# The opening schedule of a recurrent-attention and feed-forward kernel: first chunk in another order

## The chip, the cores and the metric

The kernel runs on one core of one Trainium2 chip. The metric is device time in microseconds (us) of one execution; lower is better. The kernel before takes 201.43 us, the median of three runs (201.3 to 201.53). The profiled execution has a span of 199.0 us, and all times of the trace count from its start.

## What is computed

For each of 4 batches and 8 heads the reference keeps a 48x48 state and walks through 768 steps:

```python
for t in range(S):                         # r, k, v: [4, 8, 768, 48]
    cur   = einsum('bhd,bhe->bhde', u * k_t, v_t)
    y[t]  = einsum('bhd,bhde->bhe', r_t, state + cur)
    state = w * state + einsum('bhd,bhe->bhde', k_t, v_t)
x   = y as [3072, 384]
h   = x @ w_in                             # [384, 2048]
out = (h * sigmoid(h)) @ w_out             # [2048, 384]
```

The kernel cuts the 768 steps into 6 chunks of 128. One chunk of one batch is a **unit**: unit i is chunk i // 4 of batch i % 4, so there are 24, and units 0 to 3 are the first chunk, which has no state to start from.

## The kernel before

Work on one unit goes through all engines. In program names, with the short words that the schedule uses (i is the unit):

- loads `rin`, `kin`, `vin` (`lr`, `lk`, `lv`): 192 KB each, four buffers of each kind;
- `TR`, `TK`: TensorE transposes r and k into the accumulator `att`; `rT`, `kT`: VectorE multiplies them by powers of w; `A`: TensorE forms the 128x128 products of each head; `am`: VectorE masks them;
- `ku`, `ru`: GpSimd forms k*u and r*k*u; `rd`: VectorE sums that over each head; `vu`: v times the sum, on VectorE for units 0 to 3 and on GpSimd from unit 4 on; `kc`: GpSimd's decayed k; `sd`: GpSimd's decayed state;
- `Y`: TensorE's output into `yp`; `y16`: VectorE adds `vu` and frees `yp`; `S`: TensorE's new state into `sp`; `st`: the state is put away (ScalarE for units 0 to 3, VectorE later); `stb`: GpSimd's 16-bit copy;
- `yT`, `xT`: y transposed, and copied for the feed-forward part; `L`: six TensorE matmuls with `win` into `hps`; `G`: ScalarE's silu; `i_q`, `i_o`: GpSimd asks for quarters of `win` and `wout`.

`wb`, `ub` spread the rows w and u over 128 partitions with a matmul; `ubc` copies the second into `u_bc`.

```python
att = [ps.tile([128, 2, 512], FP, name=f"att{i}") for i in range(2)]
def next_att():                            # the two accumulators take turns
    turns.append(0)
    return att[len(turns) % 2]
...
nc.scalar.dma_start(out=u_row, in_=...u as one row...)
nc.scalar.dma_start(out=w_row, in_=...w as one row...)
for i in range(B):
    for dst, src in ((rin, r), (kin, k), (vin, v)):
        ld(i, dst, src, nc.scalar if i < 2 and dst is kin else nc.sync)
...
spins = [0]
def spin(ps_tile):                         # matmuls of zeros, for nothing but to keep TensorE at work
    for _ in range(spins[0]):
        nc.tensor.matmul(ps_tile, idle[:, 0:128], idle[:, 0:ps_tile.shape[-1]], start=True, stop=True)
    spins[0] = 0
...
yp, sp, hps, ops, yT, bc:  ps.tile(..., tag="moe", bufs=4)    # four PSUM banks for all of them
```

The opening is a written list; each word is one step, and a number with a star gives the zero matmuls ahead of it. Each engine runs its own share of the list in this order:

```python
order = """
    lnw 5*TR0 eK lamK rT0 8*TK0 v160 ub kT0 A0 ubc i_q0 v161 wb am0 ku0 TR1 lnwb TK1 lamC
    rT1 Y0 i_q1 kT1 ru0 lr4 4*A1 v162 i_q2 rd0 TR2 vu0 TK2 kc0 lk4 lv4 y160 am1 ku1 yT0 S0
    ... (cut: units 1 to 5) ...
    yT4 yT5 G2.14 ru6 xT4 xT5 kc7 rd6 vu6 ku7 ru7 stb4 rd7 stb5 vu7 v167
"""
```

After it a loop takes two units at a time; `fill(n)` sets n pieces of feed-forward work between the steps:

```python
for i in range(6, 24, 2):
    product_pair(i)                        # A of units i and i+1
    for n in (i + 2, i + 3):
        bonus_products(n)                  # ku, ru on GpSimd
        decayed_k(n)                       # kc on GpSimd
    masked(i); masked(i + 1)               # am on VectorE
    fill(4)
    outputs(i); evict_y(i); turn_y_dma(i); state(i); state16(i)      # Y S, y16, xT, st, stb
    fill(2)
    outputs(i + 1); evict_y(i + 1); turn_y_dma(i + 1); state(i + 1); state16(i + 1)
    ...
    fill(2)
    for n in (i + 2, i + 3): turn(n); decay(n)
    for n in (i + 2, i + 3): bonus_sum(n); cast_v(n); bonus_v(n); decayed_state(n)   # rd, v16, vu, sd
    ...
```

Of the kernel before, what the change touches and what calls it, by code (L numbers as in the profile page):

```python
# [8 lines left out]
FP = mybir.dt.float32  # L9
# [6 lines left out]
def kernel(  # L16
# [11 lines left out]
    nc = tc.nc  # L28

    B, H, S, D = r.shape  # L30
    C = 128
    NCH = S // C
    HD = H * D
    NP = H // 2
# [9 lines left out]
    cst = ctx.enter_context(tc.tile_pool(name="cst", bufs=1))  # L44
# [9 lines left out]
    turns = []  # L54

    def next_att():
        turns.append(0)
        return att[len(turns) % 2]
# [12 lines left out]
    def ld(i, dst, src, eng=nc.sync):  # L71
        sc, b = unit(i)
        eng.dma_start(
            out=dst[i % NIN][:, :, 0:D],
            in_=src[b, :, sc * C:sc * C + C, :].rearrange("h t d -> t h d"))
# [19 lines left out]
                      in_=bass.AP(tensor=src.tensor, offset=D * j, ap=[[1, D], [PW, NP]]))  # L95

    w_row = cst.tile([1, HD], FP)
    u_row = cst.tile([1, HD], FP)
    ones = cst.tile([1, 128], FP)
    idle = cst.tile([128, 512], F16)  # L100
    nc.scalar.preload_act_table_set("natural_log_exp_and_others")
# [1 line left out]
    nc.vector.memset(idle, 0.0)  # L103
    columns(nc.sync, wpT, w, 1)
    columns(nc.scalar, wpT, w, 0)
    nc.scalar.dma_start(out=u_row, in_=bass.AP(tensor=u.tensor, offset=0, ap=[[0, 1], [1, HD]]))
    nc.scalar.dma_start(out=w_row, in_=bass.AP(tensor=w.tensor, offset=0, ap=[[0, 1], [1, HD]]))
    for i in range(B):
        for dst, src in ((rin, r), (kin, k), (vin, v)):
            ld(i, dst, src, nc.scalar if i < 2 and dst is kin else nc.sync)  # L110
    nc.vector.memset(ones, 1.0)
    for i in range(NIN):
        nc.vector.memset(rin[i][:, :, D:64], 0.0)
# [32 lines left out]

    spins = [0]

    def spin(ps_tile):
        for _ in range(spins[0]):  # L150
            nc.tensor.matmul(ps_tile, idle[:, 0:128], idle[:, 0:ps_tile.shape[-1]],  # L151
                             start=True, stop=True)
        spins[0] = 0

# [12 lines left out]

    spread = {}

    def spread_row(key, row):  # L170
        spread[key] = ps.tile([128, HD], FP, name="bc", tag="moe", bufs=4)
        nc.tensor.matmul(spread[key], ones, row, start=True, stop=True)  # L172

    def ln_w():
        nc.scalar.activation(out=lnw_bc, in_=spread["w"], func=AF.Ln)
# [4 lines left out]
        nc.scalar.activation(out=wCT, in_=lnwT, func=AF.Exp, scale=float(C))  # L180
        nc.scalar.preload_act_table_set("silu_and_others")

    def copy_u():
        nc.scalar.copy(out=u_bc.rearrange("p h d -> p (h d)"), in_=spread["u"])  # L184
        nc.scalar.copy(out=maskX[0:HC, :], in_=maskM[HC:C, :])
        nc.scalar.copy(out=maskX[HC:C, :], in_=maskM[0:HC, :])

# [2 lines left out]
    def L(i):  # L190
        return live.setdefault(i, {})
# [45 lines left out]

    def turn_one(i, x):
        if x == 0:
            t = next_att()  # L240
            spin(t[:, 0, :])
            L(i)["t"] = t.rearrange("p y (x g t) -> p y x g t", x=2, g=NP)
        else:
            spin(L(i)["t"][:, 0, 1].rearrange("p g t -> p (g t)"))
        flat = (rin, kin)[x][i % NIN].rearrange("p h d -> p (h d)")
        for p in range(NP):
            for y in range(2):
                rows = slice(HC * y, HC * y + HC)
                nc.tensor.transpose(L(i)["t"][0:PR, y, x, p, :], flat[rows, 128 * p:128 * p + PR],  # L249
                                    ident[rows, rows])  # L250
# [19 lines left out]
        nc.scalar.copy(out=L(i)["rT16"], in_=L(i)["rT"])  # L270

    def product(i):
        at = next_att()
        spin(at[:, 0, :])
        a = L(i)["a"] = at.rearrange("p j (g c) -> p j g c", g=NP)
        rT, kT = L(i)["rT"], L(i)["kT"]
        for p in range(NP):
            for j, r0 in ((0, 0), (1, 64)):
                nc.tensor.matmul(a[:, j, p, :], kT[r0:r0 + D, p, :], rT[r0:r0 + D, p, :],  # L279
                                 start=True, stop=True)  # L280
# [16 lines left out]
    def masked(i):  # L297
        am = L(i)["am"] = wrk.tile([128, 2, NP, C], F16, name="am")
        nc.vector.tensor_tensor(  # L299
            out=am.rearrange("p h g c -> p (h g) c"), in0=L(i)["a"].rearrange("p h g c -> p (h g) c"),  # L300
            in1=(maskX if crossed(i) else maskM).unsqueeze(1).broadcast_to([128, H, C]), op=ALU.mult)

    def outputs_y(i):
        sc, b = unit(i)
        yp = ps.tile([128, 512], FP, name="yp", tag="moe", bufs=4)
        spin(yp)
        L(i)["y"] = yp[:, 0:HD].rearrange("p (h d) -> p h d", h=H)
        for p in range(NP):
            if sc:
                nc.tensor.matmul(L(i)["y"][:, 2 * p:2 * p + 2, :],  # L310
                                 L(i)["rT16"][0:PR, p, :],
                                 st16[b][:, p, :], start=True, stop=False)
            for j in range(2):
                h = 2 * p + j
                nc.tensor.matmul(L(i)["y"][:, h, :], L(i)["am"][:, j, p, :], L(i)["vy"][:, h, :],  # L315
                                 start=not sc, stop=(not sc or j == 1))
# [74 lines left out]
    def l1_mm(sc, b0, nb, ft):  # L391
        m = B // nb
        hps = hpss[b0, ft] = ps.tile([128, m, nb * C], FP, name="hps", tag="moe", bufs=4)
        spin(hps.rearrange("p m c -> p (m c)"))
        for f in range(m):
            for q in range(NQ):
                nc.tensor.matmul(hps[:, f, :], win[:, q, (ft + f) * 128:(ft + f + 1) * 128],  # L397
                                 xts[sc][:, q, b0:b0 + nb, :].rearrange("p b t -> p (b t)"),
                                 start=(q == 0), stop=(q == NQ - 1))
# [37 lines left out]
    def fill(n):  # L437
        for _ in range(n):
            if fillers:
                fillers.pop(0)()  # L440
# [14 lines left out]
    def piece(word, f):  # L455
# [2 lines left out]

    steps = {
        "lnw": powers_r, "eK": exponents_k, "lamK": powers_k,  # L460
        "wb": lambda: spread_row("w", w_row), "ub": lambda: spread_row("u", u_row),
        "lnwb": ln_w, "lamC": powers_c, "ubc": copy_u,
    }
    unit_steps = {
        "TR": lambda i: turn_one(i, 0), "TK": lambda i: turn_one(i, 1),
        "rT": lambda i: decay_one(i, 0), "kT": lambda i: decay_one(i, 1),
        "A": product, "am": masked, "v16": cast_v, "kc": decayed_k,
        "vu": lambda i: bonus_v_rows(i) if i < B else bonus_v(i),
# [4 lines left out]
        "osb": lambda b: store(0, b),  # L473
    }
    order = """
        lnw 5*TR0 eK lamK rT0 8*TK0 v160 ub kT0 A0 ubc i_q0 v161 wb am0 ku0 TR1 lnwb TK1 lamC
        rT1 Y0 i_q1 kT1 ru0 lr4 4*A1 v162 i_q2 rd0 TR2 vu0 TK2 kc0 lk4 lv4 y160 am1 ku1 yT0 S0
        xT0 st0 ru1 lr5 kT2 2*Y1 rT2 1*TR3 kc1 lk5 rd1 1*A2 vu1 lv5 ku2 S1 y161 st1 ru2 lr6 am2
        yT1 xT1 kc2 lk6 rd2 3*Y2 L0.0 vu2 lv6 sd4 S2 G0.0 y162 L0.2 sd5 st2 rT3 yT2 L0.4 ku3 TK3
        G0.2 L0.6 kT3 G0.4 ru3 lr7 L0.8 G0.6 A3 i_q3 rd3 G0.8 vu3 xT2 i_o0 TR4 v163 am3 TK4 kc3  # L480
        lk7 lv7 L0.10 v164 kT4 G0.10 Y3 kc4 S3 y163 st3 TR5 rT4 ku4 yT3 TK5 rT5 xT3 ru4 r164
        L2.0 kT5 r165 L2.2 kc5 rd4 G2.0 A45 G2.2 vu4 ku5 L2.4 am4 L2.6 G2.4 ru5 am5 Y4 G2.6 S4
        sd6 L0.12 v165 y164 L2.8 sd7 st4 TR6 i_o1 G0.12 rd5 Y5 S5 G2.8 rT6 TK6 vu5 L0.14 st5
        r166 i_o2 L2.10 G0.14 y165 i_o3 kT6 G2.10 L2.12 v166 kc6 TR7 TK7 G2.12 rT7 L2.14 ku6 kT7
        r167 yT4 yT5 G2.14 ru6 xT4 xT5 kc7 rd6 vu6 ku7 ru7 stb4 rd7 stb5 vu7 v167
    """
    for word in order.split():
        if "*" in word:
            n, word = word.split("*")
            spins[0] = int(n)  # L490
        if word == "A45":
            product_pair(4)
        elif word in steps:
            steps[word]()
        elif word[0] == "L":
            piece(word[1:], l1_mm)
        elif word[0] == "G":
            piece(word[1:], l1_silu)
        elif word[0] == "M":
            l2_mm(0, int(word[1]), int(word[3]))  # L500
        else:
            unit_steps[word[:-1]](int(word[-1]))
# [5 lines left out]
    for i in range(B + 2, NU, 2):  # L508
        sc, b = unit(i)
        nxt = range(i + 2, min(i + 4, NU))  # L510
        product_pair(i)
        for n in nxt:
            bonus_products(n)
            decayed_k(n)
        masked(i)
        masked(i + 1)
        fill(4)
        outputs(i)
        evict_y(i)
        turn_y_dma(i)  # L520
        state(i)
        state16(i)
        fill(2)
        outputs(i + 1)
        evict_y(i + 1)
        turn_y_dma(i + 1)
        state(i + 1)
        state16(i + 1)
        if b:
            fillers.extend((first(sc) if sc > 1 else rest_first(sc)) + second(sc))  # L530
        fill(2)
        for n in nxt:
            turn(n)
            decay(n)
        load(i + NIN)
        load(i + 1 + NIN)
        for n in nxt:
            bonus_sum(n)
            cast_v(n)
            bonus_v(n)  # L540
            decayed_state(n)
        for n in nxt:
            fill(2)
            cast_r(n)
        fill(4)
# [31 lines left out]
```

## Time and profile before

| what | value |
|---|---|
| time, median of 3 | 201.43 us |
| span of the profiled execution | 199.0 us |
| TensorE (PE) busy | 188.1 us, 95% |
| GpSimd (POOL) busy | 117.7 us, 59% |
| ScalarE (ACT) busy | 107.9 us, 54% |
| VectorE (DVE) busy | 102.6 us, 52% |
| zero matmuls before 52.5 us | 24, 8.2 us busy |
| from 52.5 to 195.6 us (143.1 us): PE busy | 143.0 us |
| last matmul ends, last copy ends | 195.5 us, 196.1 us |

How to read it: a matmul's record overlaps that of its neighbour, so 95% does not mean that no time can be gained, and the zero matmuls count as busy. The line to keep in mind is the one from 52.5 us on: there one TensorE instruction follows the other until the end. What can be won or lost lies ahead of that point, or in new holes after it.

### The profile page before, as it was taken

What the parts mean: (1) busy time and instruction counts of PE and PEld (TensorE: products, weight loads), DVE (VectorE), ACT (ScalarE), POOL (GpSimd) and SP (SyncE); (2) the same over time, 40 slices, a digit from 0 to 9 for tenths busy, and PEclk for the clock granted to TensorE, in tenths of its full rate; (3) what the DMA queues carried; (4) which work ended last, traced back from release to release, by engine and by line L of the source; (5) the groups of instructions that cost most, each with busy time, mean ns of one, the idle gap of its engine ahead of it and who ended that gap; (6) DMA issues with size and microseconds to landing.
All of it is one profiled execution on the core that took longest, in us unless ns stands there. A gap on an engine that the chain in (4) does not pass through costs nothing.

```text
span 199.0 us, 5520 instructions
## 1 busy us (share of the span) xinstructions
PE 188.1 (95%) x2254; PEld 122.4 (61%) x2254; DVE 102.6 (52%) x176; ACT 107.9 (54%) x216; POOL 117.7 (59%) x151
## 2 busy tenths in 40 slices
PE   5899798989799999999999999999999999999992
PEld 2466476878676688666646756547665566644551
DVE  6229979673772782763564554646635625000121
ACT  5255478678572076073794355792436880179300
POOL 8079897889989919839839649569468030000000
PEclk9999999999999999999999999999999999999999
DMA  5999999899149258279175386291395102310022
GB/s 97 238 186 199 198 198 185 173 165 180 16 94 245 83 127 172 65 156 219 26 145 113 82 187 174 46 199 38 85 216 141 40 3 59 104 40 0 0 79 79
DMA packets 89981, 24.15 MB, mean 121 GB/s; under 512 B 83298, under 2 KB 89956, under 8 KB 89956
## 3 DMA queue, kind: packets, MB, share of 16 engines
q1 hardware_dynamic: 83952, 20.26, 46.7%
q0 software_dynamic: 3712, 3.15, 10.5%
q10 hardware_dynamic: 2292, 0.40, 1.0%
q8 instruction: 17, 0.28, 0.6%
q14 instruction: 8, 0.07, 0.1%
HBM read 20.45 MB, written 4.72 MB: 126 GB/s over the span
## 4 chain that ended last, share of the span: by engine, by line
PE 76%; POOL 16%; issue 4%; DVE 1%; ACT 1%; POOLq 0%; DVEq 0%
PE ops L418 32%; PE hps L397 25%; PE att L292 6%; PE att L249 5%; POOL kc L207 4%; POOL ku L199 4%; POOL rku_f L203 2%; PE yp L315 2%; POOL sdec L338 2%; PE yp L310 2%; PE bc L172 2%; POOL wout L89 2%; PE sp L327 1%; PE att L279 1%; PE att L151 1%
## 5 line engine op out<-in xcount | busy, mean ns | idle before, releaser
L397 PE MATMUL hps<-xT,win 128*128 128x256 f16 (+1 forms) x384 | 66.9, 326 | 0.4 <-ACT xT L385 0.4
L418 PE MATMUL ops<-wout,gT 128*128 128x384 f16 x384 | 65.8, 326 | 0.0
L405 ACT ACTIVATE gT<-hps 128x512 f16<-128x512 f32 x96 | 55.0, 604 | 18.3 <-PE hps L397 16.2
L418 PEld LDWEIGHTS <-gT 128*128 128x128 f16 x384 | 36.2, 98 | 23.1
L397 PEld LDWEIGHTS <-win 128*128 128x128 f16 x384 | 35.8, 98 | 23.0 <-issue 0.4
L299 DVE TENSOR_TENSOR am<-att,maskM 128x1024 f16<-128x1024 f32 x14 | 17.1, 1222 | 35.1 <-PE att L292 31.9
L424 ACT COPY osb<-ops 128x384 f32<-128x384 f32 x20 | 9.6, 480 | 45.2 <-PE ops L418 45.2
L223 POOL TENSOR_TENSOR vu<-vin,rku 128x384 f32<-128x384 f32 x20 | 16.5, 830 | 28.8 <-DVE rku L218 22.2
L199 POOL TENSOR_TENSOR ku<-kin,u_bc 128x384 f32<-128x384 f32 x24 | 24.4, 1018 | 5.8 <-ACT u_bc L184 5.4
L203 POOL TENSOR_TENSOR rku_f<-rin,ku 128x384 f32<-128x384 f32 x24 | 24.5, 1019 | 1.8
L207 POOL TENSOR_TENSOR kc<-kin,lamC 128x384 f16<-128x384 f32 x24 | 24.0, 1003 | 0.7 <-ACT wCT L180 0.7
L255 DVE TENSOR_TENSOR rT<-att,lamR 112x512 f32<-112x512 f32 x24 | 16.5, 686 | 11.6 <-PE att L249 7.4
L343 DVE TENSOR_TENSOR y<-yp,vu 128x384 f16<-128x384 f32 x24 | 13.3, 556 | 13.1 <-POOL ku L199 4.7
L255 DVE TENSOR_TENSOR kT<-att,lamK 112x512 f32<-112x512 f32 x24 | 16.3, 680 | 3.5 <-PE att L249 3.5
L292 PEld LDWEIGHTS att<-rT,kT 48*64 48x64 f32 x640 | 14.5, 133 | 3.3 <-issue 2.8
L292 PE MATMUL att<-rT,kT 48*64 48x64 f32 (+1 forms) x640 | 16.1, 247 | 0.0
L426 DVE COPY osb<-ops 128x384 f32<-128x384 f32 x4 | 2.2, 558 | 25.0 <-PE ops L418 25.0
L218 DVE TENSOR_REDUCE rku<-rku_f 128x8 f32<-128x384 f32 x24 | 12.4, 543 | 3.5 <-POOL rku_f L203 3.5
L338 POOL TENSOR_TENSOR sdec<-st,wCT 112x384 f32<-112x384 f32 x16 | 13.5, 846 | 0.4 <-ACT st L358 0.4
L270 ACT CAST rT<-rT 112x512 f16<-112x512 f32 x20 | 12.4, 623 | 0.9 <-DVE rT L255 0.8
L315 PEld LDWEIGHTS <-am 128*128 128x128 f16 x192 | 9.7, 98 | 4.8 <-DVE am L299 3.2
L299 DVE TENSOR_TENSOR am<-att,maskX 128x1024 f16<-128x1024 f32 x10 | 12.1, 1214 | 0.0
(63 smaller groups left out, 179.3 us busy)
## 6 DMA issues: line engine op xcount, KB each, us to landing
rin<-in_r_dram SPq DMA_DIRECT2D x24, 192.0 KB, 3.6
vin<-in_v_dram SPq DMA_DIRECT2D x24, 192.0 KB, 3.8
out_dram<-osb SPq DMA_DIRECT2D x24, 192.0 KB, 2.7
kin<-in_k_dram SPq DMA_DIRECT2D x22, 192.0 KB, 3.6
win<-in_moe_w_in_dram POOLq DMA_DIRECT2D x4, 384.0 KB, 6.5
wout<-in_moe_w_out_dram POOLq DMA_DIRECT2D x4, 384.0 KB, 8.2
kin<-in_k_dram ACTq DMA_DIRECT2D x2, 192.0 KB, 4.8
xT<-y SPq DMA_TRANSPOSE x18, 2.3
```

Source lines behind the costliest of these rows:

```text
L199: nc.gpsimd.tensor_tensor(out=L(i)["ku"], in0=kin[i % NIN][:, :, 0:D], in1=u_bc, op=ALU.mult)
L203: nc.gpsimd.tensor_tensor(out=L(i)["rku_f"], in0=rin[i % NIN][:, :, 0:D], in1=L(i)["ku"], op=ALU.mult)
L207: nc.gpsimd.tensor_tensor(out=kc[i % NIN][:, :, 0:D], in0=kin[i % NIN][:, :, 0:D], in1=lamC, op=ALU.mult)
L223: nc.gpsimd.tensor_tensor(out=L(i)["vu"], in0=vin[i % NIN], in1=L(i)["rku"].unsqueeze(2).broadcast_to([128, H, D]), op=ALU.mult)
L255: nc.vector.tensor_tensor(out=L(i)[key].rearrange("p g (y t) -> p y g t", y=2), in0=L(i)["t"][0:PR, :, x], in1=lam.rearrange("p g (y t) -> ...
L292: nc.tensor.matmul(a[e][o0:o0 + HC, j, p, c0:C], kT[r0:r0 + D, p, s0:s0 + HC], rT[r0:r0 + D, p, c0:C], start=True, stop=True)
L299: nc.vector.tensor_tensor(out=am.rearrange("p h g c -> p (h g) c"), in0=L(i)["a"].rearrange("p h g c -> p (h g) c"), in1=(maskX if crossed ...
L315: nc.tensor.matmul(L(i)["y"][:, h, :], L(i)["am"][:, j, p, :], L(i)["vy"][:, h, :], start=not sc, stop=(not sc or j == 1))
L338: nc.gpsimd.tensor_tensor(out=L(i)["sdec"], in0=st[b], in1=wCT.unsqueeze(2).broadcast_to([PR, NP, PW]), op=ALU.mult)
L397: nc.tensor.matmul(hps[:, f, :], win[:, q, (ft + f) * 128:(ft + f + 1) * 128], xts[sc][:, q, b0:b0 + nb, :].rearrange("p b t -> p (b t)"), ...
L405: nc.scalar.activation(out=gts[sc][:, ft:ft + m, b0 * C:(b0 + nb) * C], in_=hpss[b0, ft], func=AF.Silu)
L418: nc.tensor.matmul(opss[b], gts[sc][:, ft, b * C:(b + 1) * C], wout[:, ft, :], start=(ft == 0), stop=(ft == NFT - 1))
```

## The change

It rearranges the opening. r and k of a unit are transposed by one step, `T`. The table of u is loaded with 128 copies by a DMA straight into `u_bc` (192 KB on the queue of ScalarE) instead of one row, a matmul and a copy; so GpSimd's `ku` can begin without TensorE. On that queue v of unit 0 takes the place of k of unit 0. The zero matmuls go into the accumulator that `next_att` will hand out next, ahead of the step, and 21 of them stand in the list instead of 24 (9 ahead of `T0`, 6 ahead of `A0`). The first three quarters of `win` are asked for after `ku` and `ru` of units 0 and 1. Almost every step changes its place. And `rd` and `vu` of units 6 and 7 leave the list: they come in the loop's first round, after the masks.

```diff
-    u_row = cst.tile([1, HD], FP)
-    nc.scalar.dma_start(out=u_row, in_=bass.AP(tensor=u.tensor, offset=0, ap=[[0, 1], [1, HD]]))
+    nc.scalar.dma_start(out=u_bc, in_=bass.AP(tensor=u.tensor, offset=0,
+                                              ap=[[0, 128], [D, H], [1, D]]))
...
-            ld(i, dst, src, nc.scalar if i < 2 and dst is kin else nc.sync)
+            by_act = (i == 0 and dst is vin) or (i == 1 and dst is kin)
+            ld(i, dst, src, nc.scalar if by_act else nc.sync)
...
-    def spin(ps_tile):
+    def spin():
         for _ in range(spins[0]):
-            nc.tensor.matmul(ps_tile, idle[:, 0:128], idle[:, 0:ps_tile.shape[-1]],
+            nc.tensor.matmul(att[(len(turns) + 1) % 2][:, 0, :], idle[:, 0:128], idle,
                              start=True, stop=True)
...
     order = """
-        lnw 5*TR0 eK lamK rT0 8*TK0 v160 ub kT0 A0 ubc i_q0 v161 wb am0 ku0 TR1 lnwb TK1 lamC
-        rT1 Y0 i_q1 kT1 ru0 lr4 4*A1 v162 i_q2 rd0 TR2 vu0 TK2 kc0 lk4 lv4 y160 am1 ku1 yT0 S0
-        ... (cut)
+        lnw eK lamK 9*T0 ku0 v160 kT0 ru0 lr4 rT0 6*A0 ku1 rd0 vu0 v161 ru1 wb am0 T1 lr5 lnwb
+        i_q0 lamC kT1 2*Y0 i_q1 y160 1*T2 kc0 lk4 lv4 rT1 yT0 xT0 rd1 1*A1 i_q2 v162 vu1 kc1 lk5
+        lv5 S0 st0 am1 ku2 S1 kT2 st1 Y1 ru2 lr6 y161 rT2 1*T3 yT1 kc2 lk6 xT1 rd2 1*A2 vu2
+        lv6 ku3 S2 L0.0 am2 st2 ru3 lr7 L0.2 kc3 lk7 kT3 Y2 G0.0 L0.4 y162 G0.2 sd4 L0.6 rT3
+        G0.4 yT2 rd3 sd5 G0.6 A3 xT2 sd6 L0.8 am3 v163 mx L0.10 G0.8 vu3 lv7 i_q3 Y3 G0.10 S3
+        i_o0 y163 T4 st3 yT3 kT4 kc4 xT3 rT4 ku4 v164 L2.0 r164 L2.2 ru4 G2.0 T5 G2.2 kc5 L2.4
+        rd4 kT5 L2.6 G2.4 vu4 rT5 A45 G2.6 ku5 r165 ru5 L0.12 am4 L2.8 G0.12 sd7 am5 Y4 G2.8 S4
+        L0.14 v165 y164 L2.10 st4 L2.12 i_o1 rd5 G0.14 Y5 vu5 T6 G2.10 S5 G2.12 i_o2 y165 L2.14
+        v166 st5 yT4 i_o3 G2.14 yT5 kT6 xT4 kc6 rT6 xT5 r166 T7 ku6 kT7 ru6 rT7 r167 kc7 ku7 ru7
+        stb4 stb5 v167
     """
...
         masked(i)
         masked(i + 1)
+        if i == B + 2:
+            bonus_sum(i)
+            bonus_v(i)
+            bonus_sum(i + 1)
+            bonus_v(i + 1)
         fill(4)
```

More of the change, by code (lines that the diff above doesn't have):

```diff
@@ L168, with spread_w @@
     spread = {}
-    def spread_row(key, row):
-        spread[key] = ps.tile([128, HD], FP, name="bc", tag="moe", bufs=4)
-        nc.tensor.matmul(spread[key], ones, row, start=True, stop=True)
+    def spread_w():
+        spread["w"] = ps.tile([128, HD], FP, name="bc", tag="moe", bufs=4)
+        nc.tensor.matmul(spread["w"], ones, w_row, start=True, stop=True)
     def ln_w():
@@ L181, in powers_c, with cross_mask @@
         nc.scalar.preload_act_table_set("silu_and_others")
-    def copy_u():
-        nc.scalar.copy(out=u_bc.rearrange("p h d -> p (h d)"), in_=spread["u"])
+    def cross_mask():
         nc.scalar.copy(out=maskX[0:HC, :], in_=maskM[HC:C, :])
@@ L239, in turn_one @@
         if x == 0:
[L240 to L244, printed above, removed]
+            L(i)["t"] = next_att().rearrange("p y (x g t) -> p y x g t", x=2, g=NP)
         flat = (rin, kin)[x][i % NIN].rearrange("p h d -> p (h d)")
@@ L272, in product @@
     def product(i):
-        at = next_att()
-        spin(at[:, 0, :])
-        a = L(i)["a"] = at.rearrange("p j (g c) -> p j g c", g=NP)
+        a = L(i)["a"] = next_att().rearrange("p j (g c) -> p j g c", g=NP)
         rT, kT = L(i)["rT"], L(i)["kT"]
@@ L305, in outputs_y @@
         yp = ps.tile([128, 512], FP, name="yp", tag="moe", bufs=4)
-        spin(yp)
         L(i)["y"] = yp[:, 0:HD].rearrange("p (h d) -> p h d", h=H)
@@ L393, in l1_mm @@
         hps = hpss[b0, ft] = ps.tile([128, m, nb * C], FP, name="hps", tag="moe", bufs=4)
-        spin(hps.rearrange("p m c -> p (m c)"))
         for f in range(m):
@@ L460 @@
         "lnw": powers_r, "eK": exponents_k, "lamK": powers_k,
-        "wb": lambda: spread_row("w", w_row), "ub": lambda: spread_row("u", u_row),
-        "lnwb": ln_w, "lamC": powers_c, "ubc": copy_u,
+        "wb": spread_w,
+        "lnwb": ln_w, "lamC": powers_c, "mx": cross_mask,
     }
     unit_steps = {
-        "TR": lambda i: turn_one(i, 0), "TK": lambda i: turn_one(i, 1),
+        "T": turn,
         "rT": lambda i: decay_one(i, 0), "kT": lambda i: decay_one(i, 1),
@@ L475 @@
     order = """
-        lnw 5*TR0 eK lamK rT0 8*TK0 v160 ub kT0 A0 ubc i_q0 v161 wb am0 ku0 TR1 lnwb TK1 lamC
-        rT1 Y0 i_q1 kT1 ru0 lr4 4*A1 v162 i_q2 rd0 TR2 vu0 TK2 kc0 lk4 lv4 y160 am1 ku1 yT0 S0
[L478 to L485, printed above, removed]
+        lnw eK lamK 9*T0 ku0 v160 kT0 ru0 lr4 rT0 6*A0 ku1 rd0 vu0 v161 ru1 wb am0 T1 lr5 lnwb
[8 more added lines that the diff above has]
+        stb4 stb5 v167
     """
@@ L490 @@
             spins[0] = int(n)
+            spin()
         if word == "A45":
```

## The prediction

> **What bounds the kernel now.** I read the page's slices first: PE shows nines almost everywhere, so I asked where TensorE truly waits. The list of waits, restricted to PE after 52.5 us, is empty; so nothing after that point can be gained, and the question is when that gapless stretch begins.
>
> ```profile
> PE   5899798989799999999999999999999999999992
> POOL 8079897889989919839839649569468030000000
> DMA  5999999899149258279175386291395102310022
> ```
>
> A slice is 5 us. In the first ten POOL is at 7 to 9 and the DMA engines at 8 or 9. The chain that ended last, in order of time, says who ruled: GpSimd from 15 us to 50 us, and then this:
>
> ```profile
> 48.49 0.96 POOL ku L199
> ...
> 49.53 1.01 POOL rku_f L203
> 50.56 0.55 DVE rku L218
> 51.11 1.14 DVE am L299
> ...
> 52.30 0.22 PE yp L315 x2
> ```
>
> The last hole of TensorE closes at 52.30 us: Y6 waits for am6, which in VectorE's order stands behind rd7, which waits for ru7 of GpSimd. Four lines of the timeline show why this began late:
>
> ```profile
> 10.09 2.08 PE L279 MATMUL att<-rT,kT 48*128 48x128 f32 x16
> 10.76 1.00 POOL L199 TENSOR_TENSOR ku<-kin,u_bc 128x384 f32<-128x384 f32 x1 [5.35 <-ACT u_bc L184]
> ...
> 12.28 1.23 DVE L299 TENSOR_TENSOR am<-att,maskM 128x1024 f16<-128x1024 f32 x1 [2.90 <-PE att L279]
> ...
> 15.00 0.99 POOL L207 TENSOR_TENSOR kc<-kin,lamC 128x384 f16<-128x384 f32 x1 [0.72 <-ACT wCT L180]
> ```
>
> GpSimd sat idle 5.35 us for u_bc.
>
> **What the Trainium skill says.** "TensorE: Matmul & The Clock Gate", Part 1: the array runs at half clock until about 3.4 us of sustained work, and falls back after an idle window of about 3.4 us. The trace agrees on the halves: four zero matmuls of 512 columns take 1.88 us at 15 us, about 0.42 apart, and three take 0.81 at 23.5 us, about 0.21 apart behind the first; no hole once it is at full clock is long enough to show the falling back. "DMA: Bandwidth & Descriptors", "Issuing engines are not separate DMA queues": moving a load from one queue to another gives no bandwidth. The trace moved 239 GB/s from 5 to 10 us and about 185 to 200 until 30 us with three queues in use, which fits one shared limit. "SBUF — State Buffer", "Who interferes with whom": a VectorE operation with two SBUF inputs contends with GpSimd's reads. The tile view agrees: vu on VectorE takes 0.78 to 1.50 us, so I use 1.2.
>
> **The start, part by part.** The u table adds 192 KB, about 1 us of DMA at 195 GB/s, and takes away a spread on TensorE (two matmul passes, 1.64 us together) and a 0.48 copy on ScalarE. r0, issued at 1.42, let TensorE start at 4.55; with the u table beside it I put r0 at 5.3 and k0 at about 6.8 (one more pair of 192 KB at 239 GB/s). So T0 ends near 7.3, against 8.6 for TK0. Nine zero matmuls, 9 x 0.42 from 1.29, end at 5.1: harmless. The six ahead of A0 are 2.5 us from 7.3, still at half clock: A0 starts at 9.8, not 10.09, takes 2.0 and lets am0 start at 11.8, not 12.28. That is a choice; at full clock it would be 10.5.
>
> **First chunk.** From am0 to y16 of unit 3 VectorE has four am (1.13 from start to start), six kT/rT (0.60), three rd (0.47), three vu (1.2), four y16 (0.47): 4.5 + 3.6 + 1.4 + 3.6 + 1.9 = 15.0 us. I add 1.0 for T1, which stands behind the spread of w on TensorE (11.8 + 1.6 + 0.7 = 14.1, when am0 has ended at 13.0), and 1.5 for A3, behind four pieces L (0.65 each). y163 ends at 29.3; before, it started at 32.41 and ended at 32.95. A gain of 3.6 us by here. GpSimd is not in the way: it does ku, ru of units 0 and 1 from about 7 to 11, in time that was idle, and kc0 follows the spread of w at about 14.6.
>
> **Where the gain goes.** Two ways lead on.
> TensorE's own: from y163 the transposed copy takes 0.9, then, in the new order, four L 2.6, T5 0.5, A45 1.5, two L 1.3, Y4 and S4 0.8, three L 2.0, Y5, T6, S5 1.3, L 0.65, yT 0.4, T7 0.5, product pair 1.5: 13.05. The pair of units 6 and 7 ends at 43.3, against 48.1. Four pieces, Y6, S6, two pieces, Y7: 5.2 more, 48.5. There TensorE meets S7.
> GpSimd's way to S7: the new program puts vu6 and vu7 in the loop, after masked() in the text. On GpSimd that is *behind* ku, ru, kc of units 8 and 9, which stand above. And in the built program S7 gets the bank of yp of unit 6, so it waits for y166, which waits for vu6. So I count GpSimd forward from vu5. vu5 waits for rd5, and rd5 stands on VectorE behind am4, am5, y164, st4: y163 + 0.9 + four L and T5 3.1 + A45 1.5 + two am 2.3 + y164 0.5 + st4 0.7 + rd5 0.5 = 29.3 + 9.5 = 38.8, vu5 to 39.65. These lines give the pace from there:
>
> ```profile
> 41.35 0.83 POOL L223 TENSOR_TENSOR vu<-vin,rku 128x384 f32<-128x384 f32 x1 [0.58 <-DVE rku L218]
> ...
> 52.17 1.00 POOL L199 TENSOR_TENSOR ku<-kin,u_bc 128x384 f32<-128x384 f32 x1
> 53.25 1.00 POOL L203 TENSOR_TENSOR rku_f<-rin,ku 128x384 f32<-128x384 f32 x1
> 54.22 1.00 POOL L207 TENSOR_TENSOR kc<-kin,lamC 128x384 f16<-128x384 f32 x1
> 55.18 1.01 POOL L199 TENSOR_TENSOR ku<-kin,u_bc 128x384 f32<-128x384 f32 x1
> ```
>
> ku, ru, kc cost 3.01 us a unit. Behind vu5: two requests for wout 1.55, units 6 and 7 6.0, two stb 0.9, units 8 and 9 6.0, vu6 0.8: 15.25, so 54.9; y166 0.56; S7 at 55.5. Before, S7 ran at 54.67. **Of the 3.6 us nothing is left**: TensorE arrives at 48.5 and stands for about 7 us. Taking am6 away from behind rd7 helps Y6, but the six GpSimd operations now stand between the list and vu6.
> After such a hole the clock gate should be closed: about 3.7 us of work at half clock costs 1.8 us. Sum: 201.43 + 0.8 + 1.8 = 204.0. A hand count misses small waits, but full clock at A0 would give 1 us back; I leave both out and set 203.9.
>
> **Rivals.** (a) No hole, the schedule's aim: TensorE stays ahead, and S7 comes at 48.5 instead of 54.67: 6 us come off, 195.3. For it: TensorE really arrives earlier. Against it: the order on GpSimd and the bank of S7 are fixed in the program, and the row times give no way to do 15 us of GpSimd work faster. (b) DMA sets the pace: the slices show 8 and 9 to 50 us, and the same loads, plus 1 us, must come sooner. k7 is needed near 42 us; up to it 6.9 MB are asked for, 35 us at 195 GB/s from 3 us on, so about 38. Slack of 4 us; if it goes, 204 to 206. (c) The hole is there, but the clock stays or comes back at once: 202.2. (d) The six zero matmuls run at full clock, or k0 lands early: all of the chain moves 1 us forward, 203.
>
> **Range and chances.** S7 may fall 1.7 us either way (k0, clock at A0, VectorE against GpSimd), the clock costs 0 to 2.5. That gives 201.0 to 206.6. Faster by over 2% needs under 197.4, thus no hole at all: 0.03. Slower by over 2% needs over 205.5, thus a late chain and a full clock penalty: 0.20. Within 2%: 0.77.
>
> **What the profile after would show.** ku of unit 0 near 7 us; y163 ending near 29; PE with one long idle stretch, about 48 to 55 us, that ends with y16 and vu; GpSimd's vu6 after kc of unit 9; 256-column matmuls about twice as far apart for some 4 us after the hole; no PE wait later. A hole under 3 us, or S7 well before 53, would make me wrong, and so would a slice of PE that waits for loads.

## Result and the profile after

The changed kernel takes **207.26 us** (206.66 to 207.98, four runs) against 201.37 us of the kernel before beside it: a ratio of 1.03, 95% interval 1.026 to 1.0341. The prediction was 203.9 with 201.0 to 206.6: the direction, the hole and the operation that ends it came as counted, and the time lies outside the range. The profiled execution has a span of 206.3 us against 199.0, 7.3 more; all times below are from these two profiles unless a run is named. The two happen to be the slowest of four (207.98) and the fastest of four (200.73), so their 7.3 us are more than the 5.9 between the medians, and sums of the parts below add up to 7.3.

The slices of the page (5.16 us each here), in the order TensorE, GpSimd, granted clock, DMA:

```profile
PE   7893998988549999999999999999999999999993
...
POOL 7699687569970982974956928929839130000000
PEclk9999599999957999999999999999999999999999
DMA  3999999999008616829629239466287100320022
```

TensorE's row has two thin places that the row of before had not: a 3 in the fourth slice, and 5 and 4 in the eleventh and twelfth. After each the clock row falls to 5 (fifth slice; twelfth, and 7 in the thirteenth). In the eleventh and twelfth GpSimd has 9 and 7 while the DMA row is at 0: the work is on GpSimd, and no load is waited for.

TensorE's list of waits up to 70 us (total us, times, longest):

```profile
PE sp L320 <- DVE y L336: 5.4, 1, 5.4
PE yp L308 <- DVE am L293: 2.2, 1, 2.2
PE att L286 <- DVE rT L251: 1.5, 2, 0.8
PE att L152 <- DVE rT L251: 1.4, 2, 1.3
...
```

The first line is the hole that the prediction looked for, the second and the last are the thin fourth slice, which it did not have, and the third is two waits of 0.79 and 0.76 in the product pair of units 6 and 7. After 59.7 us the list is empty, so the rest of the program is work without a gap, as before.

The timeline around the hole (start, duration, engine, line, operation; in brackets the idle time ahead and who ended it):

```profile
42.99 0.82 POOL L223 TENSOR_TENSOR vu<-vin,rku 128x384 f32<-128x384 f32 x1 [4.00 <-DVE rku L218]
...
57.25 0.99 POOL L207 TENSOR_TENSOR kc<-kin,lamC 128x384 f16<-128x384 f32 x1
58.21 1.61 POOL L223 TENSOR_TENSOR vu<-vin,rku 128x384 f32<-128x384 f32 x2
59.07 0.56 DVE L336 TENSOR_TENSOR y<-yp,vu 128x384 f16<-128x384 f32 x1 [6.58 <-POOL vu L223]
...
59.68 0.48 PE L320 MATMUL sp<-v,kc 128*128 128x96 f16 x4 [5.35 <-DVE y L336]
```

S of unit 7 (`sp`, 59.68) waits 5.35 us for y16 of unit 6 (59.07), which waits for vu6 (58.21), and vu6 stands right behind ku, ru, kc of units 8 and 9. From the end of vu5 at 43.81 to S7 are 15.87 us; the sum of row times had given 15.85. Before, S7 ran at 54.62 without a wait:

```profile
54.62 0.33 PE L327 MATMUL sp<-v,kc 128*128 128x96 f16 x4
```

It comes 5.1 us later, and the other 2.2 of the 7.3 us are lost behind it.

### The profile page after: what moved, and what is told of

The parts are those of the page before. It is cut to its first block, busy times and chain, and to the rows that moved or that the text cites. A ratio compares the mean times of both kernels' runs of the same rounds, so it can differ in the third digit from the quotient of the medians.

```text
span 206.3 us, 5503 instructions
## 1 busy us (share of the span) xinstructions
PE 189.2 (92%) x2249; PEld 123.5 (60%) x2249; DVE 103.0 (50%) x176; ACT 107.8 (52%) x215; POOL 117.7 (57%) x151
## 4 chain that ended last, share of the span: by engine, by line
PE 73%; POOL 14%; issue 6%; DVE 3%; DMA 2%; ACT 1%; POOLq 0%; SPq 0%; DVEq 0%; ACTq 0%
PE ops L410 31%; PE hps L389 24%; PE att L286 7%; PE att L245 5%; POOL kc L207 4%; POOL ku L199 3%; POOL rku_f L203 3%; DMA rin<-in_r_dram 2%; PE yp L308 2%; PE yp L303 1%; PE sp L320 1%; PE att L152 1%; POOL sdec L331 1%; POOL vu L223 1%; POOL win L84 1%
## 5 line engine op out<-in xcount | busy, mean ns | idle before, releaser
L389 PE MATMUL hps<-xT,win 128*128 128x256 f16 (+1 forms) x384 | 68.8, 334 | 0.6 <-ACT xT L378 0.6
L389 PEld LDWEIGHTS <-win 128*128 128x128 f16 x384 | 37.1, 101 | 24.0 <-issue 0.7
L207 POOL TENSOR_TENSOR kc<-kin,lamC 128x384 f16<-128x384 f32 x24 | 24.6, 1027 | 0.4 <-ACT wCT L181 0.3
L232 ACT CAST v<-vin 128x384 f16<-128x384 f32 x24 | 11.5, 512 | 3.4 <-DMA vin<-in_v_dram 3.4
L245 PEld LDWEIGHTS att<-ident,rin 64*112 64x112 f32 x192 | 8.0, 142 | 7.6 <-issue 6.1
```

What stands on the lines that cost most here:

```text
L207: nc.gpsimd.tensor_tensor(out=kc[i % NIN][:, :, 0:D], in0=kin[i % NIN][:, :, 0:D], in1=lamC, op=ALU.mult)
```

## Experiments

Each ratio is to the kernel before on the same chip (201.1 us, or 200.97 for the last three), with its 95% interval.

### 1. Only the move of rd and vu

The kernel before, its opening kept, with `rd` and `vu` of units 6 and 7 taken from the list and put where the change puts them:

```diff
-        ... xT4 xT5 kc7 rd6 vu6 ku7 ru7 stb4 rd7 stb5 vu7 v167
+        ... xT4 xT5 kc7 ku7 ru7 stb4 stb5 v167
...
         masked(i + 1)
+        if i == B + 2:
+            bonus_sum(i); bonus_v(i); bonus_sum(i + 1); bonus_v(i + 1)
```

> The kernel before with this one part of the change: rd and vu of units 6 and 7 leave the list and follow the masks in the loop's first round, behind ku, ru, kc of units 8 and 9 on GpSimd. Theory: vu6 ends near 57.3 us, y16 of unit 6 near 57.9, S7 at 58 instead of 54.7, so plus 3.3 us, and 0 to 2 us for half clock after a hole of some 4 us: 204.7 to 206.7 us. Rival (the move is harmless or helps, since am6 no longer waits for rd7; what costs is the new order of the first chunk): 200 to 202 us.

Measured: 206.27 us, ratio 1.0291 (1.0255 to 1.0327). Its timeline has the same chain as the changed kernel:

```profile
56.28 1.61 POOL L223 TENSOR_TENSOR vu<-vin,rku 128x384 f32<-128x384 f32 x2
...
57.75 0.37 PE L327 MATMUL sp<-v,kc 128*128 128x96 f16 x4 [4.74 <-DVE y L343]
```

S7 is 3.1 us later than before, TensorE stood 4.74 us, and by windows of half a microsecond the clock is at half for 3.41 us after it. That is 1.7 us of work lost; 3.1 + 1.7 = 4.8, and the span is 203.8 against 199.0. This one move does nearly the whole damage by itself, in a kernel whose opening is otherwise untouched.

### 2. The changed kernel with the queue of GpSimd turned round

In the loop's first round, vu of units 6 and 7 go ahead of ku, ru, kc of units 8 and 9:

```diff
-        for n in nxt: bonus_products(n); decayed_k(n)
+        if i > B + 2:
+            for n in nxt: bonus_products(n); decayed_k(n)
         masked(i); masked(i + 1)
         if i == B + 2:
             bonus_sum(i); bonus_v(i); bonus_sum(i + 1); bonus_v(i + 1)
+            for n in nxt: bonus_products(n); decayed_k(n)
```

> The changed kernel with one thing moved: in the loop's first round GpSimd does vu of units 6 and 7 ahead of ku, ru, kc of units 8 and 9. Theory (the hole is made by the place of vu6 alone): vu6 ends near 53.1 us instead of 59.0, S7 runs when TensorE arrives, near 54.2 instead of 59.7, no idle TensorE and no half clock behind it; minus 5.4 us for the hole and minus 2 us for the half clock, about 200 us, some 0.99 to 1.0 of the kernel before. Rival (GpSimd has too much to do at this point whatever the order, so the wait only moves to the next product that needs it): a wait of 3 us or more within the next 10 us, 204 us or more.

Measured: 199.32 us, ratio 0.9911 (0.9879 to 0.9943). Its executions spread from 197.7 us at a mean granted clock of 0.991, over 199.3 at 0.983, to 202.3 at 0.966, which is the profiled one, so that only order and waits are read from its profile. S7 starts at 56.20 without a wait there, and no hole is left around it. So the order on GpSimd turns 207.26 into 199.32: 7.9 us. The wait of 2.2 us for am1 and the half clock behind it are still in this profile.

### 3. TensorE kept at work in the first chunk

To the changed kernel: 16 zero matmuls in a bank of their own, nine ahead of Y1 and seven ahead of T3. The kernel's own zero matmuls go into the accumulator that comes next; these go into one of the four shared banks that nobody reads in the meantime. Which of the four a later accumulator gets can change with it.

```diff
+    def spare(n):
+        z = ps.tile([128, 512], FP, name="zz", tag="moe", bufs=4)
+        for _ in range(n):
+            nc.tensor.matmul(z, idle[:, 0:128], idle, start=True, stop=True)
...
-        ... S1 kT2 st1 Y1 ru2 lr6 y161 rT2 1*T3 yT1
+        ... S1 kT2 st1 9-zeros Y1 ru2 lr6 y161 rT2 7-zeros 1*T3 yT1
```

> The changed kernel, vu of units 6 and 7 left where the change puts them, with only the 9 and 7 zero matmuls in a bank of their own ahead of Y of unit 1 and the transposes of unit 3. Theory (the prediction's count was short by the half clock in the first chunk, and by little else): clock 1.0 from 20 to 27 us, y16 of unit 3 at 29.4 as in the kernel with the zero matmuls above, every later step 2.9 us earlier than in the changed kernel, S7 near 56.8 after a hole of about 5 us; 204.0 to 204.7 us, inside the range that the prediction gave. Rival (GpSimd is late for reasons of its own, so that its chain to vu of unit 6 does not follow): above 206 us.

Measured: 204.66 us, ratio 1.0173 (1.0139 to 1.0206). Here is the first chunk of the changed kernel without them, then the windows of both. In the timeline, vu1 on VectorE, two GpSimd operations beside it, and what follows:

```profile
14.94 2.47 DVE L212 TENSOR_TENSOR vu<-vin,rku 128x384 f32<-128x384 f32 x1
...
15.02 1.01 POOL L207 TENSOR_TENSOR kc<-kin,lamC 128x384 f16<-128x384 f32 x1
...
15.98 1.00 POOL L199 TENSOR_TENSOR ku<-kin,u_bc 128x384 f32<-128x384 f32 x1
...
17.34 1.21 DVE L293 TENSOR_TENSOR am<-att,maskM 128x1024 f16<-128x1024 f32 x1
...
18.60 0.38 PE L308 MATMUL yp<-v,am 128*128 128x48 f16 x8 [2.17 <-DVE am L293]
...
20.26 0.59 PE L152 MATMUL att<-idle 128*128 128x512 f16 x1 [1.28 <-DVE rT L251]
...
22.67 2.08 PE L273 MATMUL att<-rT,kT 48*128 48x128 f32 x16
...
24.80 1.23 DVE L293 TENSOR_TENSOR am<-att,maskM 128x1024 f16<-128x1024 f32 x1 [3.11 <-PE att L273]
```

vu1 takes 2.47 us, am1 therefore starts at 17.34, Y1 waits 2.17 for it, and then the zero matmul ahead of T3 waits 1.28 more for rT2, because it writes the accumulator that rT2 still reads. The windows of the changed kernel (length in us; busy us and instructions of PE, PEld, DVE, ACT and POOL; then granted clock, DMA share, GB/s):

```profile
18.00:20.00 2.00, 0.38 (x8) 0.29 (x9) 2.00 (x4) 0.44 (x2) 2.00 (x3) 0.99 1.22 193
20.00:22.00 2.00, 1.74 (x20) 1.10 (x20) 1.65 (x3) 0.00 (x0) 1.92 (x3) 0.50 1.21 192
22.00:24.00 2.00, 2.00 (x16) 1.48 (x16) 0.00 (x0) 0.48 (x1) 2.00 (x3) 0.50 1.09 216
```

and two of them of the run with the zeros:

```profile
18.00:20.00 2.00, 1.77 (x16) 0.78 (x15) 2.00 (x4) 0.67 (x3) 2.00 (x3) 1.00 1.20 186
20.00:22.00 2.00, 2.00 (x27) 1.01 (x25) 1.90 (x3) 0.16 (x1) 1.92 (x3) 1.00 1.22 196
```

Without the zeros TensorE works 0.38 of the 2 us from 18 on, and from 20 to 26 its clock is 0.50: product A2 takes 2.08 us, where the same shape took 1.16 at full clock. With the zeros the clock stays at 1.00, although vu1 still takes 2.47, and y16 of unit 3 starts at 29.45 instead of 32.30. Here is that operation in the kernel before, in the changed kernel and in this run:

```profile
32.41 0.54 DVE L343 TENSOR_TENSOR y<-yp,vu 128x384 f16<-128x384 f32 x1
...
32.30 0.56 DVE L336 TENSOR_TENSOR y<-yp,vu 128x384 f16<-128x384 f32 x1
...
29.45 0.56 DVE L341 TENSOR_TENSOR y<-yp,vu 128x384 f16<-128x384 f32 x1
```

So of the 3.6 us that the new first chunk was to gain by this point, the changed kernel had 0.1; with the clock held open it has 3.0. The hole and the half clock behind it are both still there (S7 at 56.89 behind a wait of 5.36), and the time falls by 2.6 us to 0.8 above the predicted one.

### 4. Queue turned round and zeros

Experiments 2 and 3 together:

> As the first kernel of this set, with 9 zero matmuls ahead of Y of unit 1 and 7 ahead of the transposes of unit 3, into a bank of their own that nobody reads, so that they need not wait. Theory (TensorE idles 16.4 to 18.6 and 19.0 to 20.3 us, its clock falls to half, and A of unit 2 takes 2.1 instead of 1.2 us and the four feed-forward pieces behind it 1.1 us more): the granted clock stays at 1.0 from 20 to 27 us, am of unit 2 starts near 22.5 instead of 24.8, y16 of unit 3 some 2.5 us earlier, total 2 to 3 us below the first kernel of this set, near 197.5. Rival (VectorE and GpSimd set the pace there, TensorE's clock is slack): within 0.7 us of it.

Measured: 197.35 us, ratio 0.9831 (0.9794 to 0.9867). In the profile the clock is 1.00 until after the last matmul, y16 of unit 3 starts at 29.41, S7 at 51.61 after a wait of 0.2 us:

```profile
51.61 0.33 PE L325 MATMUL sp<-v,kc 128*128 128x96 f16 x4 [0.18 <-DVE st L352]
```

**This version beats both kernels**: S7 comes 3.0 us sooner than in the kernel before, and the span is 3.0 us shorter. It differs from experiment 3 by the order on GpSimd alone, and S7 moves by 5.3 us, the span by 7.4 (203.4 to 196.0): the hole costs 5.3, the clock behind it 2.1.

### 5. The other end of the same idle time: vu1 on GpSimd

The changed kernel with the queue turned round, and vu of unit 1 on GpSimd instead of VectorE:

```diff
-        "vu": lambda i: bonus_v_rows(i) if i < B else bonus_v(i),
+        "vu": lambda i: bonus_v_rows(i) if i < B and i != 1 else bonus_v(i),
```

> As the first kernel of this set, and vu of unit 1 is done by GpSimd instead of VectorE. In the changed kernel this operation took 2.47 us on VectorE beside kc and ku of GpSimd, where 1.2 was assumed. Theory (VectorE is the bound from 12 to 20 us, and that operation is the mis-sized term): am of unit 1 starts near 16.0 instead of 17.3, rT of unit 2 near 17.7 instead of 19.5, y16 of unit 3 one to three us earlier, total 1 to 3 us below the first kernel of this set. Rival (the half clock of TensorE at 20 to 26 us is what costs, and comes anyway): within 0.7 us of it. GpSimd's own 0.8 us more would show as a later kc of unit 1.

Measured: 198.3 us, ratio 0.9871 (0.9843 to 0.9899). vu1 takes 0.84 us on GpSimd, am1 starts at 16.29, the clock is at half for 3.4 us in the first chunk instead of 6.8, and y16 of unit 3 starts at 29.79. The time is 1.0 below that of experiment 2 (199.32); the executions of the two overlap, so the gain on the whole is not clear, and the profile is what shows the shorter chain. Then both mends at once, with five and six zeros:

> vu of units 6 and 7 ahead of units 8 and 9, vu of unit 1 on GpSimd, and 5 and 6 zero matmuls in a bank of their own: the three mends of the first set together. If the shorter VectorE chain (1.2 us) and the open clock (2.9 us) are separate gains: y16 of unit 3 near 28.2, 196.2 us. If both only keep the clock open and overlap: 197.2 to 198.2 us, no better than the zero matmuls alone.

Measured: 198.46 us, ratio 0.9859 (0.9833 to 0.9886), y16 of unit 3 at 29.06. Either mend alone brings y16 of unit 3 to 29.4 or 29.8. The 0.4 that both bring on top is not theirs: in this profile the six zeros ahead of A0 already ran at full clock (1.47 us instead of 2.74 in the other two), and am0 starts at 10.30 instead of 11.33 or 11.41. From am0 to y16 of unit 3 it is 18.1 us with the zeros, 18.4 with vu1 on GpSimd and 18.8 with both. In the profile with both, S of unit 1 waits 1.2 us for kc1, which stands behind vu1 on GpSimd, and the clock is at half for 3.4 us from 46 us on, right behind two short waits in a product pair:

```profile
43.17 0.43 PE L291 MATMUL att<-rT,kT 48*64 48x128 f32 x4 [0.79 <-DVE rT L256]
44.37 1.55 PE L291 MATMUL att<-rT,kT 48*64 48x128 f32 x60 [0.76 <-DVE rT L256]
```

What part each of the two has in the time was not tried. The two mends act on the same chain: the slow vu1 leaves TensorE idle, and behind the idle time the clock is at half.

### 6. The hole filled with zero matmuls

The changed kernel, with 24 zero matmuls between Y7 and S7 (`spins[0] = 24; spin()`), so that TensorE waits just as long, but at work:

> The changed kernel with 24 zero matmuls (512 columns, about 0.21 us each) between Y and S of unit 7, into the accumulator that is free there; nothing else moves. They fill some 5.1 of the 5.4 us that TensorE waits. Theory (the hole costs twice: once by itself, once because the clock falls to half behind it): S7 stays near 59.7, the granted clock stays at 1.0 from 58 to 66 us, the total falls by 2.0 to 2.4 us to about 205. Rival (what comes behind the hole is slow because VectorE and GpSimd are behind, not for the clock): within 0.7 us of the changed kernel's 207.3.

Measured: 204.59 us, ratio 1.0172 (1.0113 to 1.0231). TensorE's timeline:

```profile
54.19 5.34 PE L152 MATMUL att<-idle 128*128 128x512 f16 x24
59.72 0.33 PE L320 MATMUL sp<-v,kc 128*128 128x96 f16 x4 [0.20 <-DVE y L336]
```

S7 starts at 59.72, as in the changed kernel (59.68); the clock is 1.00 behind it, and the span is 204.1 instead of 206.3. So the half clock behind the hole costs 2.2 us by the spans, 2.7 by the medians. The spans are the cleaner pair, since both profiles have 6.83 us of half clock in the first chunk; three of this run's four executions have a mean clock of 0.989 and not the profile's 0.983, so they had less half clock than the profile. In the changed kernel the half clock behind the hole lasted from 57.5 to 64.3 us; 4.7 us of that lie behind S7, and half of 4.7 is 2.3.

### 7. rd5 earlier on VectorE

In the changed kernel GpSimd sits idle 4.00 us ahead of vu5 (the line at 42.99 above), for rd5, which stands on VectorE behind both am of units 4 and 5. This puts it ahead of them:

```diff
-        ... r165 ru5 L0.12 am4 ... i_o1 rd5 G0.14
+        ... r165 ru5 rd5 L0.12 am4 ... i_o1 G0.14
```

> The changed kernel with one step moved: rd of unit 5 stands on VectorE ahead of am of units 4 and 5, not behind am, y16 and st. Theory (GpSimd idled 4.0 us for that sum, and every step of its chain to vu of unit 6 followed): vu of unit 5 near 39.0 us instead of 43.0, S7 near 55.7 instead of 59.7, hole about 1.5 us instead of 5.4, no half clock behind it: 200.8 to 202 us. Rival (loads of units 6 to 9 or the transposes hold GpSimd up at once, so that the 4 us come back as other waits): 204 us or more.

Measured: 204.83 us, ratio 1.0194 (1.0164 to 1.0224): the rival's figure. GpSimd's timeline:

```profile
36.44 0.84 POOL L223 TENSOR_TENSOR vu<-vin,rku 128x384 f32<-128x384 f32 x1
...
49.37 1.00 POOL L199 TENSOR_TENSOR ku<-kin,u_bc 128x384 f32<-128x384 f32 x1 [3.63 <-DMA kin<-in_k_dram]
```

vu5 comes 6.5 us sooner, and then ku8 waits 3.63 us for k8, whose request came up on its queue only at 47.30, behind those for v7 and r8, which took 4.0 us each to issue. From the start of y16 of unit 3 to S7 it is 27.2 us here and 27.4 in the changed kernel: on the path, the edit gave nothing. What the run gained it had gained by y16 of unit 3 (29.64 against 32.30). A0 ran at 8.95 instead of 9.92, because the six zeros ahead of it already ran at full clock (1.47 us instead of 2.61); that put am0 0.5 us forward (10.61), since VectorE was at vu0 until then. vu1 took 2.07 us instead of 2.47. And the clock was later at half for 3.42 us in the first chunk instead of 6.83, which is 1.7 us of work; 0.5, 0.4 and 1.7 make 2.6 of the 2.7. The programs do not differ ahead of that point. Nor does it take the earlier rd5 to get such an opening: in the last run of experiment 5, which has the same program as the changed kernel up to vu1 and rd5 in its old place, the six zeros took 1.47 us too. The Trainium skill ("TensorE: Matmul & The Clock Gate", Part 1) says that the gate looks at a window of about 3.4 us that runs freely and is not set back when a kernel starts, so that the same work could fall differently into it; the 3.42 and 6.83 agree with one and two such windows. That this is why the two profiles differ was not tested. Mere chance does not settle it either: three of this run's four executions have a mean clock of 0.975, three of the changed kernel's four 0.967, so that most of them had less half clock here. Why stays open.

The same edit on the best version, experiment 4:

> The changed kernel with vu6 and vu7 ahead of units 8 and 9 on GpSimd, the zero matmuls in a bank of their own in the first chunk (197.35 measured), and in addition rd5 ahead of am4 and am5 on VectorE, so that GpSimd does not stand 4 us for it. Theory: with vu6 and vu7 in front no matmul waits at S7 any more, GpSimd's hole is off the path, and what ends last there is TensorE's own work: no change, 196.9 to 197.8. Rival: am6, am7 or vu6 still come late through GpSimd's ru7, and the 4 us give back 1 to 3: 194.5 to 196.5. If loads of units 8 and 9 set the pace, none of it shows and GpSimd waits for k8.

Measured: 197.43 us, ratio 0.9816 (0.9775 to 0.9857): the same time as without it.

```profile
49.33 1.62 POOL L228 TENSOR_TENSOR vu<-vin,rku 128x384 f32<-128x384 f32 x2 [3.56 <-DVE rku L223]
```

vu5 is at 36.47, and the idle time turns up again ahead of vu6, 3.56 us, now for rd6, behind the masks of units 6 and 7. S7 is at 51.53, 0.08 us from experiment 4, and TensorE waits 0.17 us for it: there GpSimd's idle time is off the path.

### 8. The u table alone

The kernel before, with u spread by the DMA; its matmul and its copy are left out, all else stays:

```diff
-    nc.scalar.dma_start(out=u_row, in_=...one row)
+    nc.scalar.dma_start(out=u_bc, in_=...128 copies of the row)
-        ... 8*TK0 v160 ub kT0 A0 ...
+        ... 8*TK0 v160 kT0 A0 ...
```

> The kernel before with only the u table by DMA (192 KB), and neither the matmul that spreads u nor its copy. Theory: the table shares the DMA rate with r0 and k0, so r0 and k0 land about 1 us later; TensorE loses the two passes of 1.64 us, so A0 stays near 10; ku0 starts when the table and k0 are there, 7 to 8 us instead of 10.76; but GpSimd's kc0 still waits for the powers of w near 15, so Y6 comes at most 1 us sooner and S7 with it. 200.3 to 201.6 us. Rival: the table costs as much as it seems in the changed kernel, where the first work comes 1.4 us later: S7 about 1 us later, 202 to 202.8. Another rival: GpSimd, which paces everything to 50 us, starts 3 us sooner and the whole chain follows: 198 to 199.

Measured: 201.68 us, ratio 1.003 (1.0016 to 1.0044).

```profile
5.98 0.68 PE L248 MATMUL att<-ident,rin 64*112 64x64 f32 x8 [2.38 <-DMA rin<-in_r_dram]
...
8.05 0.99 POOL L198 TENSOR_TENSOR ku<-kin,u_bc 128x384 f32<-128x384 f32 x1 [2.65 <-DMA kin<-in_k_dram]
...
15.75 0.99 POOL L206 TENSOR_TENSOR kc<-kin,lamC 128x384 f16<-128x384 f32 x1 [4.19 <-ACT wCT L180]
```

The first transpose starts at 5.98 instead of 4.58, so 192 KB ahead of r0 cost 1.4 us, where the prediction had 0.75 (5.3 against 4.55). ku0 starts at 8.05 instead of 10.76, but kc0, which needs the powers of w, waits until 15.75, later than before (15.00). An operation 2.7 us earlier on GpSimd brings nothing while the next one waits for something else; the table costs 0.6 us by itself (0.3 to 0.9 by the interval).

The best version with the earlier rd5, and the table asked for behind v0 instead of ahead of r0:

> As the last one, and the u table is asked for behind v0 instead of ahead of it, so that r0 and k0 have the DMA rate to themselves. Theory: r0 lands at 4.6 to 5.1 instead of 5.9, T0 and A0 follow, am0 starts 0.8 to 1.3 us sooner, ku0 a little later (the table lands near 8) without a wait for it in Y0; the chain of the first chunk moves by 0.5 to 1.2: 196.2 to 197.0 if the run before it gives 197.4. Rival: TensorE's clock opens after a given stretch of work, so an earlier T0 finds it at half speed for longer, or vu0 becomes the wait: no gain, within 0.4 us of the run before it.

Measured: 199.03 us, ratio 0.9914 (0.9887 to 0.9941), slower than the 197.43 it started from. The first transpose moves up to 5.24 with the r part, but its k part waits 2.14 us and starts at 8.05, where it had been near 7. A0 starts at 9.94, no sooner, and later Y6 waits 1.32 us for a silu of ScalarE. Of these two places of the table the changed kernel has the better one; why the silu came late was not followed up.

## Why the prediction was wrong, and where it was right

**The start: right.** The timeline of the changed kernel:

```profile
6.03 0.68 PE L245 MATMUL att<-ident,rin 64*112 64x64 f32 x8 [0.72 <-DMA rin<-in_r_dram]
...
6.79 1.00 POOL L199 TENSOR_TENSOR ku<-kin,u_bc 128x384 f32<-128x384 f32 x1 [2.25 <-DMA kin<-in_k_dram]
...
7.39 2.61 PE L152 MATMUL att<-idle 128*128 128x512 f16 x6
...
9.92 1.16 PE L273 MATMUL att<-rT,kT 48*128 48x128 f32 x16
```

ku0 at 6.79 (near 7 predicted). r0 came later than set (transposes at 6.03, not 5.3), and T0 ends at 7.46, near the 7.3 counted. The six zeros run at 0.42 apart, at half clock, and A0 starts at 9.92 (9.8). It takes 1.16 us and not 2.0: the clock opened at the end of the zeros. am0 starts at 11.13, 0.7 earlier than predicted.

**The first chunk: this step failed.** "y163 ends at 29.3" came out as 32.86. From am0 on, the sum of 15.0 plus 1.0 plus 1.5 us was 4.2 too short. The sum had the VectorE operations in a row, each at its usual time, and TensorE's work at full clock. Three terms were mis-sized or missing:

- vu at 1.2 us: vu1 took 2.47, beside GpSimd's kc and ku, where the kernel before has 0.78 to 1.50. An average was used, and the maximum sat on the path. The trace agrees with what the prediction cites of interference: vu1 ends 0.35 us into ru2, the third GpSimd operation beside it, which took 1.21 us instead of 1.00, while vu0 and vu2, beside one GpSimd operation and the start of the next, took 0.92 and 0.98. In experiment 8, with the table late, vu1 ran beside no product of GpSimd and took 0.56.
- TensorE's clock in the first chunk: taken as full, it was 0.50 for 6.8 us. The prediction looked for the gate only at the large hole and did not ask what happens around Y1, where the new order leaves TensorE 2.17 and 1.28 us without work. No single idle stretch there is as long as the 3.4 us that the prediction cites from the skill; the two with 0.37 us of work between them were enough, and the measurement decides. Experiment 3 measures this term: 2.85 us of the 3.6, and 2.6 of the 3.4 us by which the time missed the figure.
- T3 and its zero matmul stand ahead of A2 on TensorE and wait for rT2. From that zero matmul to A2 the trace has 2.4 us at half clock, and 1.4 (20.57 to 21.95) in experiment 3 at full clock: that much the sum had left out.

With the clock held open, the same program has y16 of unit 3 ending at 30.0, against 29.3 by the sum: 0.7 us is what remains of the slow vu1 and T3, once the earlier am0 is set against them. The next edge was near enough: rd5 ends 10.0 us after y163 instead of 9.5.

**The way of GpSimd: right.** vu6 behind kc9, 15.9 us from the end of vu5 to S7 (15.85), S7 released by y16 of unit 6. Add up the errors on this way: 0.7 early at am0, 4.2 late over the first chunk, 0.6 late at rd5 and vu5, give S7 at 59.6 by 55.5 + 4.1; measured 59.68. That the time missed the figure by 3.4 and not by 4.1 and more is luck and no merit of the sum: it comes of the 1.4 us by which the two profiles lie farther apart than the medians.

**The hole: right in kind, a quarter shorter.** 5.35 us instead of about 7, because TensorE itself arrived at 54.3, 5.8 later than counted; 3.6 of these come from the first chunk, and 1.55 are the two waits in the product pair of units 6 and 7, which the sum for TensorE had left out. That shortens the hole and does not move its end.

**The clock behind the hole: right in kind, low by 0.3 to 0.5.** 1.8 us were set for 3.7 us at half clock; it was 4.7 us, because the half clock lasts 6.83 us and begins 2.2 us ahead of the end of the hole. 2.2 are left when S7's shift is taken off the span, and experiments 4 and 6 give 2.1 and 2.2.

**The rivals.** (a), no hole, is what experiment 2 and above all experiment 4 made of it: 197.35 and not 195.3, because S7 comes at 51.61 there and not at 48.5. (b), the DMA, does not act in the changed kernel, where TensorE waits for no load after T0; it does in experiment 7, as soon as GpSimd is 6.5 us earlier. (c), a clock that stays, did not come by itself; it takes a filled hole, and is then worth 2.2 to 2.7 us (experiment 6). (d), zeros at full clock, came half true in the changed kernel, where A0 but not the zeros ran at full clock and the 0.7 us gained went under in the rest; in the profile of experiment 7 it came true, with am0 at 10.61, 1.2 us ahead of the predicted 11.8.

In short, the loss is the order of six GpSimd operations; experiment 1 shows it in the kernel before, and experiment 2 takes it away. What the prediction had lost sight of is that the gain of 3.6 us ahead of it was counted at full clock, and that in the new order the clock was at half there for 6.8 us.

## What to carry to other kernels

When work moves from a written order into a loop, count where it lands in each engine's queue, not where its consumer stands: six operations in front of one small one cost 5 us here, and turning them round gave 7.9 back. Sum a chain with TensorE's clock as a term of its own: look for every place in the new order where it goes short of work in short stretches one after the other (2.17 and 1.28 us here, and in one run 0.79 and 0.76), not only for the large hole, and put filler matmuls into a bank that nobody reads, or they wait with the rest. And before an operation that waits is pulled forward, look for what it would wait for next: twice here (rd5, the u table) the idle time only moved.

## What the runs showed of the hardware that was not expected

- The half clock comes in portions: summed over windows of half a microsecond it lasts 3.41 us in experiment 1, 3.42 in the first chunk of experiments 5 (vu1 on GpSimd) and 7 and behind 46 us in experiment 5 with both mends, and 6.83 in the changed kernel, at both thin places. A portion costs up to 1.7 us, less where part of it falls into idle time.
- Two idle stretches of 2.17 and 1.28 us with 0.37 us of work between them were enough for it, and two portions of it followed although TensorE had work without a pause from 20.3 us on. In the profile of experiment 5 with both mends, 0.79 and 0.76 us with 0.43 us of work between them came before one portion; the same two waits in the changed kernel and in experiment 4 brought none. So the length of an idle stretch alone did not decide it; what does was not found.
- One VectorE product of 128x384 with two inputs in SBUF took between 0.55 us (vu3 in experiment 2) and 2.48 (vu1 in experiment 4), while the two GpSimd operations beside the latter kept their 1.01 and 1.00 and the third took 1.21.
- Filler work in a hole cost next to nothing: 24 zero matmuls moved S7 by 0.04 us and took 2.2 us off the span.
